# Linear attention in chunks of 64 instead of 128 tokens: scores as four 64x64 array tiles, half the mask, states by one scan

## The chip, the cores and the metric

The kernel runs on one core of a Trainium2 chip, in fp32. The metric is the device time of one execution in microseconds (us). Wherever a ratio is given, it is the mean time of a kernel's fast runs over the mean of the unchanged kernel's fast runs of the same rounds on the same chip, with a 95% interval; it is therefore not quite the ratio of the medians quoted beside it.

## The reference, cut to what matters

```python
# attention: 4 batches, 8 heads, 768 tokens, 48 columns a head
f = 1.0 / (1.0 + np.exp(-f_logit))
for t in range(S):
    state = f[:, :, t, :, None] * state + np.einsum('bhd,bhe->bhde', k[:, :, t], v[:, :, t])
    y[:, :, t] = np.einsum('bhd,bhde->bhe', q[:, :, t], state)
# the heads side by side are x (4, 768, 384); the mixer follows
h = xt @ U @ V                                   # along the tokens, rank 32
u = x + h.transpose(0, 2, 1)
ch = np.maximum(u @ w_ch1, 0.0) @ w_ch2          # 384 -> 1536 -> 384
return u + ch
```

The kernel cuts the tokens into chunks. Inside a chunk the recurrence is a masked product (scores, then inner product); between chunks a 48x48 state is carried on. Gates enter as running products: keys are multiplied by a product X that is scanned backwards over the chunk, queries by its inverse-like Y.

## The kernel before: what the change and the argument touch

Two heads of one batch make a unit; there are 16 units, four to a batch. A unit's work on TensorE comes in pieces, and the pieces of a later batch are dealt out between the mixer's matmuls of the batch before. The kernel is written in one order, and a scheduler fixes at build time in which order the instructions stand on each engine; an engine then takes its list in that order.

```python
C = P                                   # 128 tokens a chunk; NCH = 6 chunks

def scores(g):                          # g = 0, 1: three chunks each
    for c in range(G):
        for par in range(2):            # the two heads
            nc.tensor.matmul(sc[:, par, c * C : (c + 1) * C],
                lhsT=T["k"][rows[par], chunk[g * G + c]], rhs=T["q"][rows[par], chunk[g * G + c]], ...)
    nc.vector.tensor_tensor(T["A"][...], sc[...], causal..., ALU.mult)        # mask

def states():
    ...                                 # 10 products of 128 tokens into ds
    nc.vector.tensor_tensor(st, ds[...], T["whole"]..., ALU.mult)
    for c in range(2, NCH):             # one small update per chunk
        nc.vector.scalar_tensor_tensor(st[:, c - 1, :], st[:, c - 2, :], T["whole"][:, c : c + 1], st[:, c - 1, :], ...)

def read():                             # y = q . state, then y += A . v, both in one piece
    ...

# gates of a later batch: transposed by VectorE, then two sigmoids on ScalarE
turned(fT, r["f"])
nc.scalar.activation(by_chunk[:, :, 1:C], fv[:, :, 1:C], AF.Sigmoid)
nc.scalar.activation(f0, fv[:, :, 0], AF.Sigmoid)

# mixer, first product: relu on ScalarE; pm is one of two PSUM buffers
nc.scalar.activation(z[a, i], pm[:, 0:HALF], AF.Relu)

order = [gates, kept, keep, keys, scores, states, read_back, queries, scores2, read]
```

(Cuts are marked by dots. `kept` transposes the keys, `read_back` scans Y, `keep` scans X.)

## Time and profile before

| what, kernel before | value |
|---|---|
| median of 4 runs | 589.89 us (589.7 to 591.07) |
| profiled run: span, mean granted TensorE clock | 589.1 us, 0.953 |
| first long second-layer piece of the mixer (end of the first stage) | starts at 114.96 us |
| first low-rank piece of the 2nd, 3rd, 4th mixer | 198.01, 336.38, 464.38 us |
| stretches between these marks, and to the end | 83.1, 138.4, 128.0, 124.7 us |
| TensorE's wait for relu, whole run | 16.3 us (12.6 before first-layer, 3.7 before second-layer matmuls) |

The marks cut the run into stretches that can be compared between kernels, since each mark stands for the same work (before the first one, 72 first-layer matmuls of the mixer and units 0 to 3 are done in every kernel; of unit 4 about 0.9 us of pieces, not always the same ones). The second and third stretch hold the same work too, four units and one mixer each, with other preparation on VectorE beside it; yet one is 10 us longer than the other.

### The profile page before, as it was taken

What the parts mean: (1) busy time and instruction counts of PE and PEld (TensorE: products, weight loads), DVE (VectorE), ACT (ScalarE), POOL (GpSimd) and SP (SyncE); (2) the same over time, 40 slices, a digit from 0 to 9 for tenths busy, and PEclk for the clock granted to TensorE, in tenths of its full rate; (3) what the DMA queues carried; (4) which work ended last, traced back from release to release, by engine and by line L of the source; (5) the groups of instructions that cost most, each with busy time, mean ns of one, the idle gap of its engine ahead of it and who ended that gap; (6) DMA issues with size and microseconds to landing.
All of it is one profiled execution on the core that took longest, in us unless ns stands there. A gap on an engine that the chain in (4) does not pass through costs nothing.

```text
span 589.1 us, 8824 instructions
## 1 busy us (share of the span) xinstructions
PE 550.6 (93%) x3737; PEld 344.2 (58%) x3737; DVE 244.8 (42%) x367; ACT 121.8 (21%) x260; POOL 62.4 (11%) x59
## 2 busy tenths in 40 slices
PE   5798897799989999989969999999999999999996
PEld 4687553457656556646645556566566555555553
DVE  5768769826697340638361620254211020000000
ACT  2233346502322103210112102120022003201200
POOL 2111125500022000113020200022000000000000
PEclk9557799999999999989998999999999999999998
DMA  9699827614652135133340310010000000000000
GB/s 167 145 225 177 189 59 208 150 35 104 164 128 54 43 83 132 42 79 94 100 107 0 87 41 13 1 21 14 28 1 1 15 13 14 1 13 27 2 14 31
DMA packets 75295, 41.56 MB, mean 71 GB/s; under 512 B 65774, under 2 KB 68846, under 8 KB 75246
## 3 DMA queue, kind: packets, MB, share of 16 engines
q1 hardware_dynamic: 75246, 40.91, 29.7%
q8 instruction: 31, 0.51, 0.4%
q14 instruction: 18, 0.15, 0.1%
HBM read 36.18 MB, written 4.72 MB: 69 GB/s over the span
## 4 chain that ended last, share of the span: by engine, by line
PE 80%; DVE 11%; DMA 3%; SPq 2%; ACT 1%; issue 1%; POOL 0%; DVEq 0%; ACTq 0%; POOLq 0%
PE po L158 32%; PE pz L149 26%; PE sc L404 5%; PE y L467 4%; PE pu L133 3%; PE pt L326 3%; DVE w_y L62 2%; DMA w_raw<-in_moe_V_dram 2%; PE y L458 2%; PE ds L430 2%; PE put L142 2%; DVE w_y L63 1%; SPq L232 1%; DVE X L358 1%; DVE Y L375 1%
## 5 line engine op out<-in xcount | busy, mean ns | idle before, releaser
L149 PE MATMUL pz<-uT,w 128*128 128x384 f32 x576 | 199.2, 497 | 13.1 <-ACT z L152 12.6
L158 PE MATMUL po<-w,z 128*128 128x384 f32 x576 | 192.2, 492 | 3.7 <-ACT z L152 3.7
L149 PEld LDWEIGHTS pz<-uT,w 128*128 128x128 f32 x576 | 106.3, 191 | 85.7 <-ACT z L152 12.9
L158 PEld LDWEIGHTS po<-w,z 128*128 128x128 f32 x576 | 109.0, 191 | 80.6 <-issue 5.9
L161 DVE TENSOR_TENSOR o<-x,po 128x384 f32<-128x384 f32 x24 | 13.3, 555 | 204.7 <-PE po L158 204.7
L152 ACT ACTIVATE z<-pz 128x384 f32<-128x384 f32 x96 | 46.8, 489 | 167.0 <-PE pz L149 167.0
L410 DVE TENSOR_TENSOR A<-sc,causal 128x768 f32<-128x768 f32 x32 | 30.3, 947 | 63.2 <-PE sc L404 63.2
L358 DVE TENSOR_TENSOR_SCAN X<-fz,ends 128x768 f32<-128x768 f32 x16 | 28.1, 1755 | 33.1 <-ACT fz L347 23.9
L341 POOL TENSOR_TENSOR kT<-kT,X 128x768 f32<-128x768 f32 x8 | 14.6, 1820 | 243.4 <-DVE kT L307 243.4
L404 PE MATMUL sc<-qT,kT 48*128 48x128 f32 x384 | 38.9, 312 | 0.2 <-DVE kT L338 0.2
L404 PEld LDWEIGHTS sc<-qT,kT 48*128 48x128 f32 x384 | 29.6, 204 | 14.2 <-issue 11.2
L467 PE MATMUL y<-v_nat,A 128*64 128x48 f32 x768 | 31.0, 245 | 0.0
L64 POOL TENSOR_TENSOR w<-w_y,w_r 128x384 int32<-128x384 int32 x24 | 23.9, 995 | 65.1 <-DVE w_y L63 65.1
L375 DVE TENSOR_TENSOR_SCAN Y<-fz,starts 128x768 f32<-128x768 f32 x16 | 28.1, 1756 | 5.8 <-POOL qT L341 5.2
L467 PEld LDWEIGHTS y<-v_nat,A 128*64 128x64 f32 x768 | 28.5, 159 | 1.7 <-issue 0.3
L473 ACT COPY x<-y 128x576 f32<-128x576 f32 x16 | 10.2, 636 | 61.2 <-PE y L467 61.2
L458 PE MATMUL y<-st,qT 48*64 48x48 f32 x640 | 18.0, 242 | 5.0 <-DVE st L441 3.6
L144 ACT COPY uT<-put 128x384 f32<-128x384 f32 x24 | 10.7, 480 | 53.7 <-PE put L142 53.7
L458 PEld LDWEIGHTS y<-st,qT 48*64 48x64 f32 x640 | 13.9, 149 | 13.0 <-issue 5.0
L62 DVE TENSOR_SCALAR w_y<-w_y 128x384 uint32<-128x384 uint32 (+1 forms) x27 | 20.3, 752 | 0.7
L133 PE MATMUL pu<-h,V 128*128 128x384 f32 x48 | 19.4, 514 | 0.8 <-DVE x L134 0.8
L341 POOL TENSOR_TENSOR qT<-qT,Y 128x768 f32<-128x768 f32 x8 | 17.2, 2156 | 17.8 <-DVE X L365 11.7
(61 smaller groups left out, 338.0 us busy)
## 6 DMA issues: line engine op xcount, KB each, us to landing
w_raw<-in_moe_w_ch_dram SPq DMA_DIRECT2D x24, 384.0 KB, 3.7
v_nat<-in_v_dram SPq DMA_DIRECT2D x32, 144.0 KB, 2.8
out_dram<-o SPq DMA_DIRECT2D x24, 192.0 KB, 1.9
f_raw<-in_f_logit_dram SPq DMA_DIRECT2D x31, 142.0 KB, 3.1
k_raw<-in_k_dram SPq DMA_DIRECT2D x31, 142.0 KB, 3.4
q_raw<-in_q_dram SPq DMA_DIRECT2D x31, 142.0 KB, 3.3
f_raw<-in_f_logit_dram SPq DMA_DIRECT2D x16, 144.0 KB, 4.9
k_raw<-in_k_dram SPq DMA_DIRECT2D x16, 144.0 KB, 5.0
```

The costliest lines, as they stand in the source:

```text
L62: nc.vector.tensor_scalar(y, y, 3, 0x3FFFFFFF, ALU.logical_shift_left, ALU.bitwise_and)
L133: nc.tensor.matmul(pm[:, 0:DM], lhsT=V[:, t * P : (t + 1) * P], rhs=h[0], start=True, stop=True)
L149: nc.tensor.matmul(pm[:, 0:HALF], lhsT=w1[:, m, i * P : (i + 1) * P], rhs=uT[a][:, m, :], start=(m == 0), stop=(m == NDC - 1))
L152: nc.scalar.activation(z[a, i], pm[:, 0:HALF], AF.Relu)
L158: nc.tensor.matmul(pm[:, 0:DM], lhsT=z[a, i][:, s * P : (s + 1) * P], rhs=w2[:, i, :], start=(i == 0), stop=(i == NFC - 1))
L341: nc.gpsimd.tensor_tensor(t, t, T[of], ALU.mult)
L358: nc.vector.tensor_tensor_scan(backwards(X, S - 1, S), backwards(f, S, S), backwards(ends, S - 1, S), 0.0, ALU.mult, ALU.add,)
L375: nc.vector.tensor_tensor_scan(Y, f[:, 0:S], starts, 0.0, ALU.mult, ALU.add)
L404: nc.tensor.matmul(sc[:, par, c * C : (c + 1) * C], lhsT=T["k"][rows[par], chunk[g * G + c]], rhs=T["q"][rows[par], chunk[g * G + c]], sta ...
L410: nc.vector.tensor_tensor(T["A"][:, :, g * G : (g + 1) * G, :], sc[:, :, 0 : G * C].rearrange("p h (c i) -> p h c i", i=C), causal.unsquee ...
L458: nc.tensor.matmul(o(a, par, c), lhsT=T["q"][rows[par], c * C + a * HC : c * C + (a + 1) * HC], rhs=T["st"][rows[par], c - 1, :], start=(c ...
L467: nc.tensor.matmul(o(a, par, c), lhsT=T["A"][:, par, c, halves[a]], rhs=vt[:, c, par, :], start=False, stop=True, skip_group_check=True,)
```

## The change

The intent: a chunk of 64 tokens halves the masked triangle, so the scores take half the multiplications, and 64x64 tiles of the array work four at a time. More chunks mean more states, so the per-chunk updates are replaced by a single VectorE scan with the chunks innermost. The order in which pieces are handed over changes as well, and the inner product becomes a piece of its own. The product for the chunk states (`ds`) also leaves the two PSUM buffers (the memory that TensorE writes to) that it shared with the mixer.

```diff
-    C = P
+    C = P // 2
...
+            whole = wholes[n % 2]                         # first chunk's factor is 0: the scan restarts there
+            nc.vector.tensor_tensor(whole[:, 1:NCH], T["f0"][:, 1:NCH], X0[:, 1:NCH], ALU.mult)
+            nc.scalar.copy(T["whole"], whole.unsqueeze(1).broadcast_to((P, D, NCH)))
...
+            for c in range(NBL):                          # scores: four tiles
+                for par in range(2):
+                    for s in range(2):
+                        nc.tensor.matmul(sc[part[s], par, c * C : (c + 1) * C],
+                            lhsT=T["k"][rows[par], chunk[2 * c + s]], rhs=T["q"][rows[par], chunk[2 * c + s]], ...)
...
-            ds = ps_mm.tile([P, 512], F32, name="ds", tag="mm")       # one of the mixer's two PSUM buffers
+            ds = ps_big.tile([P, 2, 512], F32, name="ds", tag="big")
...
-            for c in range(2, NCH):
-                nc.vector.scalar_tensor_tensor(st[:, c - 1, :], ...)
+            nc.scalar.copy(d[:, 1:]..., ds[...])          # "added", chunks innermost
+            nc.vector.tensor_tensor_scan(st, d[:, 0 : D * NCH], T["whole"]..., 0.0, ALU.add, ALU.mult)
+            T["st"] = st.rearrange("p (e c) -> p c e", c=NCH)
...
+            seen = two.tile([P, 2], F32, name="seen")     # read, then a small copy that inner waits for
+            nc.scalar.copy(seen, y[:, :, (NBL - 1) * D])
+        def inner():
+            for c in reversed(range(NBL)):
+                for par in range(2):
+                    for s in range(2):                    # two tiles, on the diagonal
+                        nc.tensor.matmul(o(s, par, c), lhsT=T["A"][part[s], par, c, :], rhs=vt[part[s], c, par, :], ...)
...
-                order = [gates, kept, keep, keys, scores, states, read_back, queries, scores2, read]
+                order = [gates, kept, keep, keys, states, scores, read_back, read, queries, inner]
```

(Comments are added here; lines are joined and cut.)

## The prediction

> **What bounds the kernel now.** I read the page's busy shares and slices first, then a table of windows, then the order of TensorE's work, and last the stage before 115 us. Slices of TensorE, VectorE and granted clock:
>
> ```profile
> PE 550.6 (93%) x3737; PEld 344.2 (58%) x3737; DVE 244.8 (42%) x367; ACT 121.8 (21%) x260; POOL 62.4 (11%) x59
> ...
> PE   5798897799989999989969999999999999999996
> ...
> DVE  5768769826697340638361620254211020000000
> ...
> PEclk9557799999999999989998999999999999999998
> ```
>
> From slice 8 on TensorE is full. The windows put numbers to it (window, length, busy time by engine, clock, DMA share, GB/s):
>
> ```profile
> 26.00:52.00 26.00, 23.50 (x298) 19.50 (x300) 19.81 (x39) 8.70 (x19) 3.58 (x4) 0.63 1.11 224
> 52.00:74.00 22.00, 19.81 (x244) 14.69 (x244) 16.90 (x31) 8.32 (x19) 3.40 (x4) 0.74 0.87 166
> ...
> 86.00:113.00 27.00, 20.72 (x62) 10.82 (x60) 26.04 (x43) 17.41 (x38) 13.51 (x14) 1.00 0.74 195
> 113.00:208.00 95.00, 91.61 (x790) 58.02 (x789) 56.59 (x73) 17.59 (x39) 10.92 (x7) 1.00 0.34 82
> 208.00:346.00 138.00, 131.32 (x899) 79.61 (x898) 61.88 (x74) 24.45 (x53) 16.04 (x8) 0.98 0.31 80
> 346.00:474.00 128.00, 128.00 (x900) 78.23 (x898) 31.82 (x52) 19.98 (x40) 7.25 (x4) 1.00 0.04 13
> ```
>
> There are three stages. Up to 74 us the first four units (two heads each) alternate between TensorE at a low clock and VectorE. From 86 to 113 us VectorE converts weights without a pause (26.04 of 27 us). From 113 to 474 us TensorE sets the pace, and units 4 to 15 lie there as small pieces between mixer matmuls; after 474 us there is no attention. So in the long stage only TensorE time counts, and VectorE work removed there is worth nothing by itself. The order of one unit in it, in TensorE's own timeline (start, length, line, output and inputs, tile, count):
>
> ```profile
> 430.39 0.80 PE L458 MATMUL y<-st,qT 48*64 48x48 f32 x40
> 431.12 1.61 PE L467 MATMUL y<-v_nat,A 128*64 128x48 f32 x48
> 432.65 2.20 PE L149 MATMUL pz<-uT,w 128*128 128x384 f32 x6
> 434.79 0.53 PE L422 MATMUL pt<-ident,kT 64*128 64x64 f32 x10
> 435.25 2.20 PE L149 MATMUL pz<-uT,w 128*128 128x384 f32 x6
> 437.38 0.94 PE L404 MATMUL sc<-qT,kT 48*128 48x128 f32 x12
> 438.25 2.20 PE L149 MATMUL pz<-uT,w 128*128 128x384 f32 x6
> 440.38 0.79 PE L430 MATMUL ds<-v_nat,kb 128*64 128x48 f32 x20
> 441.10 0.48 PE L404 MATMUL sc<-qT,kT 48*128 48x128 f32 x2
> 441.51 2.20 PE L149 MATMUL pz<-uT,w 128*128 128x384 f32 x6
> ```
>
> I take a piece's cost from its start to the next start, as ends overlap: read through the state 0.73 us, inner product 1.53, key transposes 0.46, six of twelve score products 0.87 (so 1.74 for all), chunk states 0.72. Together 5.18 us a unit. Every fp32 product is two instructions (384 score instructions are 16 units x 12 products x 2).
>
> **What the skill says.** "TensorEngine Tiling (Array Packing)", Key Properties: different tiles can load weights and multiply in parallel, and a change of tiling mode drains the engine. Both show: six mixer matmuls run in 1.94 us when more of them follow (24 in 7.74), but take 2.13 us (435.25 to 437.38) ahead of a tiled piece, and two score instructions alone cost 0.41 us. "TensorE: Matmul & The Clock Gate", LDWEIGHTS (loading the stationary operand), says that a load's time goes with its columns, at 1.2 columns a ns. The trace agrees with the first, not with the figure: the inner product, two column tiles across all 128 rows, needs 1.53 us for 48, or 26.7 ns each after some 0.25 us of switching, which is 0.42 ns a column of a 64-column load. At half clock the same x48 takes 2.73 and x24 takes 1.45 us: 53 ns each, twice as much. "PSUM — Partial Sum Buffer", PSUM bank collisions raise a hardware error, quotes that different row tiles cannot use one bank at the same time; no row of before tests it. "SBUF — State Buffer", Door 1 (its note on cachelines), says that fp32 reads a line apart (16 bytes) pay a penalty; before reads contiguously, so no run shows it yet.
>
> **A rule for pieces.** A moving column takes 0.84 ns (384 in 322 ns; a 128-column transpose 108 ns). A piece costs about 0.2 us of switching plus, for each instruction, the larger of two: load columns x 0.42 ns over the row halves that load in parallel, and moving columns x 0.84 ns over the tiles in parallel. It returns what is measured: score group 12 x max(27, 54) + 0.2 = 0.85 (0.87); states 20 x 26.7 + 0.2 = 0.73 (0.72); read 40 x max(13.4, 10) + 0.2 = 0.74 (0.73); key transposes 10 x 27 + 0.2 = 0.47 (0.46).
>
> **The change part by part, TensorE, one unit at full clock.**
> Scores: 24 products of 64x64, so 48 instructions on four tiles, 64 moving columns: max(13.4, 13.4) ns. 48 x 13.4 + 0.2 = 0.85 us for 1.74: saves 0.89.
> Inner: still 48 instructions, but 64x64 on the two diagonal tiles: the loads go in two row halves (13.4), the multiplications on two tiles (48 x 0.84 / 2 = 20). 48 x 20 + 0.2 = 1.17 for 1.53: saves 0.36.
> States: twelve chunks instead of five, 48 instructions for 20, on four tiles instead of two: 48 x 13.4 + 0.2 = 0.85 for 0.72: costs 0.13.
> Read: 44 instructions for 40, 0.79 us if nothing else changes. But the state is now read 48 bytes apart; if a moving column takes twice as long it is 44 x 20 + 0.2 = 1.08. I take 0.95, between the two: costs 0.22.
> Key transposes (one instruction each): 12 for 10 at 27 ns: 0.52 for 0.46, costs 0.06.
> Sum 4.34 for 5.18: 0.84 us a unit, and over twelve units in the long stage 10.1 us. The number of separate pieces stays five (read and inner part, the two score groups join), so the drains on the mixer's side stay. The split of the second score group (two ahead of a mixer piece, ten after) occurs some five times in the long stage at about 0.4 us; one score piece may lose it: 1 us as an expectation.
>
> **VectorE, ScalarE.** Removed: one mask of 0.947 us, one product of 0.401 and four updates of 0.266 (2.41 in all); added: one scan of 576, sized from 768 in 1.755 us as about 1.35. VectorE wins 1.06 us a unit. ScalarE gets a broadcast copy of 576 (about 0.63), a copy of 576 out of PSUM (0.65 to 1.2, strided), a token copy (0.2) and a slightly longer key copy: some 1.7 us a unit, 27 us in all, for an engine at 21%.
>
> **Before 115 us.** Here TensorE's clock was 0.50 from 30 to 40 us, and the chain of waits runs through it:
>
> ```profile
> 31.51 1.58 PE sc L404 x12
> 33.09 1.24 PE ds L430 x20
> 34.33 1.47 PE pt L326 x6
> 35.80 1.58 PE sc L404 x12
> ```
>
> Tiled pieces double at that clock, so unit 1 wins about twice the figure above, some 2 us. Unit 0 ends in a wait on a transfer of V (the chain shows 11.3 us of it), so I count nothing there. Units 2 and 3 have VectorE on the chain: 1.06 us less each, but the scan now waits for two copies of ScalarE behind the small products (about 0.5 us), plus a cheaper inner product. About 1.2 each. Sum 4.5 us. The weight conversion from 86 us starts that much earlier, as its transfers wait for VectorE and not the reverse (the queue waited 32.6 us for VectorE's conversion), so the gain carries through.
>
> **What is given back.** Before, the chunk updates ran beside other TensorE work. Now states, copy, scan (0.7 + 1.35 + 0.15 us) must end before the read, with one score piece (0.85) as sure cover: 1.4 us of wait where no mixer piece falls between. That is only while the long 24-matmul pieces are handed out, when several calls pass without any: I expect two such units, 2.8 us, and some three short waits of 0.4 us for the token copy and the mask ahead of inner. Before lost about 0.5 us in two units likewise (read 1.19 instead of 0.73). Net 3.2 us.
>
> **Sum.** 589.8 - 10.1 - 1 - 4.5 + 3.2 = 577.4; I say 577.5 us.
>
> **Rivals.** First: the diagonal tiles of inner write one bank from two row halves. If the hardware serialises them, each instruction takes 40 ns: 2.1 us instead of 1.17, 0.95 us a unit more, about 13 us over the kernel: 590, no change. The outputs are on different partitions, which speaks against it. Second: small pieces are bound by issue, not by the array. 48 score and 48 state instructions at 18 ns instead of 13.4 cost 0.45 us a unit, 6 us in all: 583. The read of before, 40 instructions in 0.73 us, speaks against it. Third: ScalarE, being in order, holds the mixer's relu behind copies that wait for VectorE. Its present copy of the scan's result already waits 32.5 us in total without much harm (TensorE waited 12.6 us for relu, with two PSUM buffers); the new one waits about 0.4 us longer. I give it 3 us: 580. Fourth, the other way: the strided read is free and no read stalls: 571.
>
> **Range and chances.** The known terms give 577; the rivals reach from 571 to 590 and mostly lie above. The 8-in-10 range is 569 to 587. The 2% mark is 578, close to the estimate: faster 0.52, within 2% 0.42, slower 0.06, the last needing serialised tiles and more waits together.
>
> **What will show it.** In the timeline after: the score piece x48 near 0.85 us (over 1.1 and the issue rival holds), inner x48 near 1.17 (over 1.5 and the bank rival holds), read x44 between 0.8 and 1.1 with the stride, states x48 near 0.85. In the waits: read behind the scan, a few us in total; the relu wait near 13 us. VectorE's busy time should fall by 17 us to about 228, ScalarE's rise to about 149. The first long mixer piece, now at 114.96 us, should start near 110.5. I am wrong if the pieces shrink as computed and the end does not follow, or if the start of that piece does not move.

## The result, and the profile after

The changed kernel takes 571.74 us (median of 4 runs, 570.41 to 572.7) for 589.89 us: ratio 0.9687, 95% interval 0.9662 to 0.9711. It is faster by 3.1%. The range of the prediction holds it; its centre, 577.5, is 5.8 us too high. Measured by profiled spans, 589.1 became 571.0: 18.1 us less.

The busy totals of the changed kernel's page:

```profile
PE 532.8 (93%) x4665; PEld 332.4 (58%) x4665; DVE 231.5 (41%) x287; ACT 145.7 (26%) x308; POOL 61.8 (11%) x64
```

TensorE has 17.8 us less to do, VectorE 13.3 us less, and ScalarE 23.9 us more (forecast: 17 less and 27 more for the last two). The windows of the changed kernel, to be laid beside those of the kernel before:

```profile
113.00:208.00 95.00, 94.95 (x1005) 59.69 (x1004) 57.02 (x64) 23.90 (x53) 11.30 (x8) 1.00 0.39 96
208.00:346.00 138.00, 137.39 (x1201) 83.11 (x1199) 59.16 (x55) 33.31 (x71) 16.08 (x8) 1.00 0.29 77
346.00:474.00 128.00, 126.67 (x1106) 75.94 (x1105) 28.27 (x32) 24.78 (x51) 7.26 (x4) 1.00 0.04 13
```

TensorE is now busy for 94.95 of 95 us and 137.39 of 138, where it had 91.61 and 131.32, and its clock is 1.00 where it was 0.98. So some 9.4 us of idle time went from these two windows (1.75 us of it is the wait that ends at the first mark, 114.96 us). That is a second source of gain beside the smaller pieces, and the prediction has no term for it. (Of the 1.33 us that are missing in the last window, 1.2 are four waits of the last mixer's preparation at 468 to 472 us; in the kernel before they come at 487 to 490 us, behind the window.)

Next, one unit in TensorE's timeline (start, length, line, operation, output and inputs, tile, shape, count):

```profile
413.50 1.60 PE L493 MATMUL y<-v_nat,A 64*64 64x48 f32 x48
415.04 2.20 PE L149 MATMUL pz<-uT,w 128*128 128x384 f32 x6
...
419.82 0.92 PE L447 MATMUL ds<-v_nat,kb 64*64 64x48 f32 x48
420.67 2.20 PE L149 MATMUL pz<-uT,w 128*128 128x384 f32 x6
422.80 0.93 PE L417 MATMUL sc<-qT,kT 48*64 48x64 f32 x48
423.66 2.20 PE L149 MATMUL pz<-uT,w 128*128 128x384 f32 x6
425.79 1.23 PE L475 MATMUL y<-st,qT 48*64 48x48 f32 x44
426.95 0.91 PE L149 MATMUL pz<-uT,w 128*128 128x384 f32 x2
```

From start to next start, states take 0.85 us and scores 0.86, both as forecast (0.85). The read takes 1.16 instead of 0.95, and the inner product 1.54 instead of 1.17: its old length (1.53).

Then the idle time. On the page, the group of the mixer's first-layer matmuls ends with the idle time ahead of it and what ended most of that. Kernel before:

```profile
L149 PE MATMUL pz<-uT,w 128*128 128x384 f32 x576 | 199.2, 497 | 13.1 <-ACT z L152 12.6
```

Changed kernel:

```profile
L149 PE MATMUL pz<-uT,w 128*128 128x384 f32 x576 | 199.7, 497 | 6.2 <-ACT z L152 5.3
```

The prediction expected this wait to stay near 13 us or to grow by 3. It fell to 5.3, and no wait for relu is left after 113 us (the 3.7 us ahead of the second-layer matmuls are gone too). The largest of those that went lies in the kernel before at 309 us; here its timeline across engines:

```profile
306.09 2.06 DVE L307 STREAM_TRANSPOSE fT<-f_raw 128x768 f32<-128x768 f32 x1
308.19 0.84 ACT L353 ACTIVATE fz<-fT 128x762 f32<-128x762 f32 x1 [6.56 <-DVE fT L307]
308.93 0.47 ACT L152 ACTIVATE z<-pz 128x384 f32<-128x384 f32 x1
309.46 3.66 PE L149 MATMUL pz<-uT,w 128*128 128x384 f32 x6 [4.71 <-ACT z L152]
```

Read it from below. TensorE stood still for 4.71 us because both PSUM buffers of the mixer were full and relu had not emptied one. Relu had its input, but ScalarE's list had the sigmoid of the next unit's gates in front of it, and ScalarE had been idle for 6.56 us waiting for that sigmoid's input, a transposition that VectorE reached late. And the pause cost more than itself: the six matmuls after it took 3.66 us, at a granted clock of 0.58, where six ahead of a tiled piece otherwise take 2.20. The kernel before has two more such waits behind its first stage, of 1.64 us (at 176 us) and 1.96 us (at 257 us). After the second of these, 24 second-layer matmuls took 9.70 us instead of 8.01, at a clock of 0.82. That is 8.3 us of waiting and 3.2 us of slow work behind it, 11.5 us in all. (At 176 us it was not a sigmoid that stood in front of the relu but `least`, a small copy of the scan X that waited for the scan.) The changed kernel at the same place, on ScalarE:

```profile
308.03 0.48 ACT L152 ACTIVATE z<-pz 128x384 f32<-128x384 f32 x1
...
309.94 0.83 ACT L362 ACTIVATE fz<-fT 128x756 f32<-128x756 f32 x1 [1.43 <-DVE whole L377]
```

Here relu stands ahead of the sigmoid. Nothing in the diff asks for that. It was the first thing to test.

### The profile page after: what moved, and what is told of

Its sections match the earlier page's. It is cut to its first block, busy times and chain, and to the rows that moved or that the text cites. A ratio compares the mean times of both kernels' runs of the same rounds, so it can differ in the third digit from the quotient of the medians.

```text
span 571.0 us, 10691 instructions
## 1 busy us (share of the span) xinstructions
PE 532.8 (93%) x4665; PEld 332.4 (58%) x4665; DVE 231.5 (41%) x287; ACT 145.7 (26%) x308; POOL 61.8 (11%) x64
## 4 chain that ended last, share of the span: by engine, by line
PE 79%; DVE 10%; DMA 2%; SPq 2%; ACT 2%; issue 2%; POOL 1%; POOLq 0%; DVEq 0%; ACTq 0%
PE po L158 33%; PE pz L149 27%; PE y L493 4%; PE pu L133 3%; PE y L475 3%; PE pt L335 2%; PE ds L447 2%; DMA f_raw<-in_f_logit_dram 2%; DVE X L367 2%; PE sc L417 2%; DVE Y L386 2%; PE put L142 1%; DVE w_y L62 1%; SPq L233 1%; DVE kT L316 1%
## 5 line engine op out<-in xcount | busy, mean ns | idle before, releaser
L161 DVE TENSOR_TENSOR o<-x,po 128x384 f32<-128x384 f32 x24 | 13.3, 554 | 206.9 <-PE po L158 206.9
L152 ACT ACTIVATE z<-pz 128x384 f32<-128x384 f32 x96 | 46.4, 489 | 125.7 <-PE pz L149 125.7
L460 DVE TENSOR_TENSOR_SCAN st<-added,whole 128x576 f32<-128x576 f32 x16 | 21.6, 1351 | 58.8 <-ACT added L454 58.8
L475 PE MATMUL y<-st,qT 48*64 48x48 f32 x704 | 21.0, 272 | 14.4 <-DVE st L460 10.9
L493 PEld LDWEIGHTS y<-v_nat,A 64*64 64x64 f32 x768 | 28.3, 156 | 7.8 <-issue 3.2
L493 PE MATMUL y<-v_nat,A 64*64 64x48 f32 x768 | 30.4, 241 | 0.2
L475 PEld LDWEIGHTS y<-st,qT 48*64 48x64 f32 x704 | 18.2, 165 | 19.7 <-issue 19.7
L144 ACT COPY uT<-put 128x384 f32<-128x384 f32 x24 | 10.9, 483 | 49.7 <-PE put L142 49.7
L447 PEld LDWEIGHTS ds<-v_nat,kb 64*64 64x64 f32 x768 | 14.1, 135 | 10.4 <-issue 7.3
L59 ACT ACTIVATE w_y<-w_raw 128x384 f32<-128x384 f32 (+1 forms) x27 | 14.8, 549 | 16.6 <-POOL w L64 9.3
```

The source lines that it names most:

```text
L447: nc.tensor.matmul(ds[par * PAD : (par + 1) * PAD, s, c * D : (c + 1) * D], lhsT=T["kb"][part[s], par, c, :], rhs=vt[part[s], c, par, :], ...
L475: nc.tensor.matmul(o(c % 2, par, c // 2), lhsT=T["q"][rows[par], chunk[c]], rhs=T["st"][rows[par], c, :], start=(c <= 2), stop=False, skip ...
L493: nc.tensor.matmul(o(s, par, c), lhsT=T["A"][part[s], par, c, :], rhs=vt[part[s], c, par, :], start=False, stop=True, skip_group_check=True,)
```

## The experiments

Theories for the 18.1 us. **Tiles**: the smaller pieces won it, as the prediction computes, and something else closed the gap. **Schedule**: the change moved the scheduler's order, which took the relu waits away, and the tile arithmetic won less than forecast. Then smaller questions: why the read and the inner product are too long, and why the first stage won so little (113.73 for 114.96 us; the forecast was 110.5).

| run | what it is | median us | ratio (95%) |
|---|---|---|---|
| x1 | before, with the changed order of pieces | 584.22 | 0.987 (0.984 to 0.990) |
| x2 | before, sigmoid of the gates held back | 577.83 | 0.976 (0.973 to 0.979) |
| x3 | changed, state read contiguously (wrong result) | 570.19 | 0.964 (0.961 to 0.967) |
| x4 | changed, state scan ahead of the Y scan | 573.72 | 0.970 (0.967 to 0.973) |
| x5 | changed, half the moving columns in inner (wrong) | one look | |
| x6 | changed, inner's outputs in two banks (wrong) | one look | |
| x7 | changed, sigmoid held back | 571.56 | 0.966 (0.962 to 0.969) |
| x8 | x7, state first in early units, state copied | 569.03 | 0.961 (0.957 to 0.964) |
| x9 | changed, 48 stationary columns in inner (wrong) | one look | |
| x10 | changed, once more | 573.72 | 0.971 (0.968 to 0.974) |
| x11 | x7 with the state copied only | 570.9 | 0.964 (0.961 to 0.968) |
| x12 | x11, state first in all units | 575.5 | 0.973 (0.970 to 0.976) |

The kernel before had medians of 591.69 (x1 to x4), 591.65 (x5 to x8) and 590.84 us (x9 to x12) beside them. The kernels marked wrong give a wrong result, because only the length of one piece was wanted of them.

### x1: the order of the pieces alone

The kernel before keeps its chunks of 128, but hands its pieces over in the changed order.

```diff
-                order = [gates, kept, keep, keys, scores, states, read_back, queries, scores2, read]
+                order = [gates, kept, keep, keys, states, scores, read_back, read, queries, inner]
```

(`scores` does both groups here, and `read` is split into read and inner.)

> The kernel before with its chunks of 128, where only the order of one unit's pieces is that of the changed kernel: states, both score groups, backward scan, read through the state, queries, inner products. Piece theory (the 18 us come from smaller TensorE pieces): 589 to 591 us, nothing gained. Schedule theory (they come mostly from waits of the mixer's matmuls for their relu, 8.3 us idle in three places plus about 3.5 us of lowered clock after two of them, which vanished because ScalarE's and VectorE's instructions came out in another order): 577 to 582 us, and the TensorE idle ahead of the mixer's matmuls after 113 us under 2 us.

Measured: 584.22 us, ratio 0.987, so some 7.5 us less, a miss of what was expected by 2 us. The waits for relu behind the first mark (114.23 us) fell from 8.3 to 3.6 us, not under 2; none is longer than 1.85. From the first mark to the end the run is 6.3 us shorter. No tile was changed, but the score groups are joined here too: in the second stretch the tiled pieces take 0.8 us less. So order alone brings about half of what the relu waits cost (12.2 us by x2), not all of it.

### x2: the gates' sigmoid held where it was written

The kernel before, with one thing changed: the two sigmoids of later batches are held to their place in program order, so that the scheduler can't move them ahead of relus written earlier.

```diff
-            nc.scalar.activation(by_chunk[:, :, 1:C], fv[:, :, 1:C], AF.Sigmoid)
-            nc.scalar.activation(f0, fv[:, :, 0], AF.Sigmoid)
+            tc.keep_in_program_order(nc.scalar.activation(by_chunk[:, :, 1:C], fv[:, :, 1:C], AF.Sigmoid))
+            tc.keep_in_program_order(nc.scalar.activation(f0, fv[:, :, 0], AF.Sigmoid))
```

> The kernel before with one thing changed: from the third batch on the sigmoid of the gates stays in program order on ScalarE, so it cannot stand ahead of a relu that TensorE waits for. Schedule theory: the two long waits (4.7 and 2.0 us) and the lowered clock after each are gone, 578 to 581 us. Piece theory: 589 to 591 us. If holding the sigmoid delays the forward scan, a wait of TensorE for it shows up instead, and the time stays.

Measured: 577.83 us, ratio 0.976. The window of the stretch that had 6.7 us of idle TensorE:

```profile
208.00:346.00 138.00, 138.00 (x931) 83.77 (x930) 60.08 (x75) 24.01 (x51) 14.55 (x8) 1.00 0.30 79
```

TensorE is busy for all 138 us. No matmul waits for relu after the start of the first long piece. Its marks are 114.49, 195.63, 323.83, 451.84 and 576.4 us, so the stretches are 81.1, 128.2, 128.0 and 124.6: the second has lost its 10 us and is now as long as the third. From the first long piece to the end, 474.1 us became 461.9: 12.2 us, against the 11.5 us counted above from waits and slow clock. The schedule theory holds, and it is the larger part: two calls on two instructions of the old kernel bring two thirds of what the whole change brought (by the ratios, 2.4 of 3.1%).

### x7: the same hold in the changed kernel

The same two lines in the changed kernel.

> The changed kernel with the gates' sigmoid held in program order on ScalarE from the third batch on, as in the run that held them in the kernel before (ratio 0.976 there). Schedule theory: in the changed kernel the waits for a relu are already small (about 1.5 us after 113 us), so at most 2 us are won: ratio 0.965 to 0.970. The ratio of this run to that one is then the worth of the tile part alone: 0.990 to 0.994 (3.5 to 6 us).

Measured: 571.56 us, 0.966, with its interval over that of the changed kernel (0.9687). The hold wins nothing that is clear of noise, because the changed kernel's own order had already put relu first. (The trace shows about 1 us: the second stretch takes 125.7 instead of 126.7 us. In the changed kernel the token copy `seen` stands behind the sigmoid twice, and TensorE's loads for the inner product wait 0.73 us for it, at 241.03 and 310.88 us; with the hold it runs at once.) Beside x2 it also measures what the change brings when the gates are held in both kernels: 0.9656 over 0.9758 is 0.9895, so about 1.05%, or 6 us. Each ratio is known to about 0.3%, so this is 6 us give or take 2; from the first mark to the end the traces show 5.9.

### x3: does the strided read of the state cost?

The changed kernel, with the state read as if its 48 columns lay side by side, instead of 48 bytes apart.

```diff
-            T["st"] = st.rearrange("p (e c) -> p c e", c=NCH)
+            T["st"] = st.rearrange("p (c e) -> p c e", c=NCH)
```

> The changed kernel with the read through the state taking 48 neighbouring values instead of values 48 bytes apart (a wrong result on purpose; the same instructions, tiles and waits). If the stride makes the read's moving operand slow: read of 44 from 1.17 to 0.79 us at full clock, 12 units x 0.38 = 4.6 us in the long stage and perhaps 1 us before it, 566 to 568 us. If the read is bound by something else (issue, bank sharing): read stays at 1.17 and the time at 571 to 572 us.

The result is wrong (relative error 0.40). TensorE's timeline:

```profile
161.06 0.90 PE L475 MATMUL y<-st,qT 48*64 48x48 f32 x44
161.90 0.88 PE L335 MATMUL pt<-ident,q_raw 128*128 128x128 f32 x6
```

The piece takes 0.84 us instead of 1.17. With 0.25 us for the change of mode, an instruction has 21 ns with the stride and 13.4 without, so the stride, and nothing else, makes the read long. At half clock (0.50 granted, in the first stage) the piece takes 1.45 us to the next start with and without the stride: there it costs nothing. In total 570.19 us, 0.964. The changed kernel did not run in these rounds, so the total is not compared; by the marks (112.82, 191.41, 317.67, 442.59 us) the three stretches with units are 2.8 us shorter than the changed kernel's, where 0.33 us in twelve units would be 4.0. That was less than expected of it, and the total of 566 to 568 us was missed.

### x5, x6, x9: why the inner product did not get shorter

Three theories for 1.53 instead of 1.17 us. The multiplications could set it (then half the moving columns shorten it), the common PSUM bank of the two diagonal tiles could (then two banks shorten it), or the loading of the stationary columns.

x5 moves 24 columns instead of 48:

```diff
-                            o(s, par, c), lhsT=T["A"][part[s], par, c, :], rhs=vt[part[s], c, par, :],
+                            y[part[s], par, c * D : c * D + (D // 2 if c else D)], lhsT=T["A"][part[s], par, c, :],
+                            rhs=vt[part[s], c, par, 0 : (D // 2 if c else D)],
```

> The changed kernel with the inner products of chunks 2 to 11 of a head taking 24 moving columns instead of 48 (a wrong result on purpose; the first two chunks keep 48 so that the whole output is written). The inner piece of 48 instructions measured 1.53 us where the forecast was 1.17. If weight loads of the two diagonal tiles go one after the other (64 columns x 0.42 ns = 26.7 ns each): it stays at 1.5 us. If the multiplications or writes into one shared bank set it: 0.25 + 8 x 26.7 + 40 x 13.4 ns = 1.0 us.

Its timeline:

```profile
168.63 1.60 PE L493 MATMUL y<-v_nat,A 64*64 64x24 f32 x48
```

The next piece starts at 170.16 us, so this one still takes 1.53 us. The multiplications do not set it. (The granted clock is 1.00 here in all three looks, so the pieces can be compared although the state of these runs is unknown.)

x6 puts the outputs of the second 64 tokens into the other bank:

```diff
-                return y[part[s], par, c * D : (c + 1) * D]
+                return y[part[s], (par + s) % 2, c * D : (c + 1) * D]
```

> The changed kernel with the outputs of the second 64 tokens of each pair put into the other bank (the heads of those tokens are exchanged, a wrong result on purpose), so that the two diagonal tiles of the inner products never write one bank at once. Bank theory: inner piece from 1.53 to about 1.17 us at full clock. Load theory: it stays at 1.5 us. The read through the state then has its row tiles in shared banks: if sharing costs, it rises above 1.17 us.

Its timeline:

```profile
168.48 1.60 PE L493 MATMUL y<-v_nat,A 64*64 64x48 f32 x48
170.01 2.20 PE L149 MATMUL pz<-uT,w 128*128 128x384 f32 x6
```

Again 1.53 us. The bank is not the cause, although the prediction had said that a piece over 1.5 us would mean just that. The second test of this run agrees: the read, whose row tiles now share banks, still takes 1.17 us (164.57 to 165.74).

x9 takes 48 instead of 64 stationary columns, and keeps the 24 moving ones:

```diff
-                            o(s, par, c), lhsT=T["A"][part[s], par, c, :], rhs=vt[part[s], c, par, :],
+                            y[s * C : s * C + (48 if c else C), par, c * D : c * D + (D // 2 if c else D)],
+                            lhsT=T["A"][part[s], par, c, 0 : (48 if c else C)],
+                            rhs=vt[part[s], c, par, 0 : (D // 2 if c else D)],
```

> As the run with half the moving columns, where the inner piece stayed at 1.53 us, so neither multiplications nor banks set it; now those products also load 48 stationary columns instead of 64 (40 of the 48 instructions; wrong result on purpose). If the loads of the two diagonal tiles go one after the other at 0.42 ns a column: 0.25 + 8 x 26.7 + 40 x 20 ns = 1.26 us. If each instruction holds its tile for a fixed 53 ns whatever its columns (two tiles in turn: 26.7): it stays at 1.53 us.

Its timeline:

```profile
168.34 1.33 PE L493 MATMUL y<-v_nat,A 64*48 64x24 f32 x48
169.61 2.20 PE L149 MATMUL pz<-uT,w 128*128 128x384 f32 x6
```

1.27 us, where 1.26 was expected. Forty of the 48 instructions have 16 columns fewer, and 0.26 us over 640 columns is 0.41 ns for each. So the load of stationary columns sets this piece, at 26.7 ns for each load of 64 columns, and not a fixed time per instruction, and the move from two tiles of 128 rows to two of 64 rows left that as it was.

What that means for the rule is argued, not shown. The runs fit two readings: either the loads of the two diagonal tiles go one after the other at 0.42 ns a column, or each tile takes 0.84 ns a column and the tiles in use work side by side. The second needs no exception for the other products: with two tiles in use a load of 64 columns comes every 26.7 ns (inner, in both kernels; states before), with four every 13.4 ns (scores and states after; the read when contiguous), and both are 53.4 ns a tile. It doesn't fit the key transposes, which load 128 columns into each of two tiles every 27 ns. The run that would separate the two, an inner product spread over all four tiles, was not made.

### x4: the first stage

The read waits for the state's scan. This is the first stage of the changed kernel, VectorE and TensorE in one timeline:

```profile
45.17 1.76 DVE L386 TENSOR_TENSOR_SCAN Y<-fz,starts 128x768 f32<-128x768 f32 x1
46.85 1.33 DVE L460 TENSOR_TENSOR_SCAN st<-added,whole 128x576 f32<-128x576 f32 x1
48.33 1.52 PE L475 MATMUL y<-st,qT 48*64 48x48 f32 x44 [3.84 <-DVE st L460]
```

The next unit's scan of Y stands ahead of the state's scan, so TensorE waits 3.84 us. Over the run these waits are 10.9 us, in three places, all before 115 us (in the kernel before, the read waits 3.2 us for the state in the same three units). x4 puts the Y scan behind the state's scan of the unit before by a dependency:

```diff
+            if n - 1 in scanned:
+                behind(ins, scanned[n - 1])
...
+            scanned[n] = nc.vector.tensor_tensor_scan(
```

> The changed kernel with VectorE's state scan held ahead of the next unit's backward scan. In the changed kernel TensorE waits 3.2 to 3.8 us for the state scan in each of units 1 to 3, and its clock falls to half for what follows. If that order is what ate the gain forecast for the stage before 115 us: these waits fall by about 1.7 us each, the first long mixer piece starts some 4 to 5 us earlier than at 113.73, total 566 to 568 us. If that stage is bound by the loop of all engines together, or by the weight conversion after it: start within 1.5 us of 113.73, total 570 to 572 us.

Measured: 573.72 us, 0.970: the same as the changed kernel, and not the 566 to 568 us expected. The three waits fell from 10.9 to 6.1 us, and the first stage's attention ended 3.7 us earlier (first low-rank piece at 64.83 instead of 68.53 us). The first mark moved from 113.73 to 106.66 us, although the last two of those matmuls then waited until 114.88 for a weight; the second mark moved by 3.7 us, from 193.67 to 189.99. But the stretch after that mark took 129.2 instead of 126.7 us, with three waits for relu of some 0.9 us again, and at the end next to nothing of the gain was left. So the order of the two scans is shown to be the cause of the first stage's small gain, and the cure moved the order elsewhere.

### x8, x11, x12: a version that beats both

x8 joins what had worked: the held sigmoids, the state first only in the units of the first stage, and from the fifth unit on a copy on GpSimd that lays the state out contiguously, for the read. Its result is correct.

```diff
+            if n - 1 in scanned and n < HP:
+                behind(ins, scanned[n - 1])
...
+            if n >= HP:
+                flat = d[:, 1:].rearrange("p (c e) -> p c e", c=NCH)
+                nc.gpsimd.tensor_copy(flat, T["st"])
+                T["st"] = flat
```

> A correct kernel meant to beat both: the changed kernel with the gates held, the state scan ahead of the backward scan in the first units only, and from unit 4 on the state copied by GpSimd into neighbouring values, so that the read runs at the contiguous 0.84 us. Expected: 4 us from the read, 3.5 us from the first stage (which the run with the state scan first everywhere won there and lost again to later waits), 0 to 1 from the held gates: ratio 0.954 to 0.959, 563 to 566 us. If GpSimd's copy comes too late the read waits for it, and most of the 4 us go.

Measured: 569.03 us, 0.961 (0.957 to 0.964). It misses what was expected of it, and it is the lowest correct time; its interval overlaps that of x11, and that of x7 at its edge. TensorE waited 1.8 us for the new copy, in three places. The first stage brought only 1.7 us at the first mark, where 3.5 were expected, and the edit says why: `n < HP` leaves out unit 4, whose Y scan (57.87 us) still stands ahead of the state's scan of unit 3 (59.54 us), so one of the three waits stays at 3.84 us.

x11 is x8 without any change of VectorE's order:

> The changed kernel with the gates held and the state copied by GpSimd into neighbouring values from unit 4 on, without any change to VectorE's order. The read at 0.84 instead of 1.17 us gives 12 x 0.33 = 4 us, less about 0.6 us where the copy is waited for (three times in the combined run): 3 us under the changed kernel of this job, ratio 0.961 to 0.964.

Measured: 570.9 us, 0.964, beside 573.72 us for the changed kernel in the same rounds. So the hold and the contiguous read together bring about 3 us, about as expected. By the marks of x7 and x11 the hold has a good part of it: the three stretches with units take 331.2 us in x7 and 330.4 in x11, so there the contiguous read wins 0.8 us net of the waits for the copy (1.9 us).

x12 has the state first in every unit, not only in the early ones:

> As the run before it, and the state scan held ahead of the backward scan in every unit (the gates are held too, so the late waits that ate this gain in the earlier run should not come back). Expected 2 to 4 us under the run before it: ratio 0.955 to 0.960. If the first stage gives nothing by this: the same time as the run before it.

Measured: 575.5 us, 0.973, a clear miss. TensorE waits 7.6 us for the copy on GpSimd, up to 3.2 us at once. The copy itself got slower. In x11, and then in x12:

```profile
280.77 1.20 POOL L466 COPY added<-st 128x576 f32<-128x576 f32 x1 [9.36 <-DVE st L460]
281.29 2.57 POOL L476 COPY added<-st 128x576 f32<-128x576 f32 x1 [13.46 <-DVE st L470]
```

In x12 VectorE's next instruction is the Y scan, and the copy runs beside it: eleven of the twelve copies take about 2.6 us there. The one without a Y scan beside it takes 1.21, and in x8 and x11, where none has one beside it, all twelve take about 1.2. What the two engines share was not tested.

### x10: the changed kernel again

> The changed kernel itself, as the reference of this job: ratio 0.966 to 0.971 to the kernel before, as on record.

Measured: 573.72 us, 0.971 (0.968 to 0.974), on another chip than x1 to x8. It agrees with the first comparison (0.9687), and the two intervals overlap. Differences of 0.3% between batches of runs are therefore not read here.

## Why the prediction was right or wrong

Direction and range were right. But two errors stood against each other, and the sum of 18.1 us has another make-up than the forecast of 12.4. That the centre is off by no more than 5.8 us is luck: the terms it did forecast brought about 5.8 us (-4.6 and -1.2 in the table), which alone would have given some 584 us, not 577.5 and not faster by 2%.

| part | forecast us | measured us, from the marks |
|---|---|---|
| smaller pieces in the long stage | -10.1 and -1 | -4.6 (changed against x2) |
| first stage | -4.5 | -1.2 |
| given back by new waits, long stage | +3.2 | about 1 for `seen`, inside the -4.6; none for the scan |
| relu waits and the slow clock behind them | not in the sum | -12.2 (x2 against before) |
| sum | -12.4 | -18.0 |

**Steps that held.** Scores (0.86 for 0.85 us), states (0.85), key transposes (0.51 for 0.52), the size of the scan (1.351 for 1.35 us) and the added ScalarE work (23.9 for 27 us). The issue rival falls with the scores and states.

**The term that was missing.** "Its present copy of the scan's result already waits 32.5 us in total without much harm (TensorE waited 12.6 us for relu, with two PSUM buffers)" is where the prediction had the answer before it and passed on. It took the relu wait for a constant of the kernel, to which the change could only add ("I give it 3 us"). The runs show that most of it in the long stage was an accident of order, worth 12.2 us with the slow clock behind it: x2 removes it on the old kernel by holding two instructions, x1 removes about half of it by the order of pieces, and the changed kernel has none left behind its first stage, with the hold or without it. The window in the prediction's own fence, 131.32 us of work in 138, was the trace of it, and so were digits in its row of slices: "From slice 8 on TensorE is full" passes over an 8, an 8 and a 6 in slices 11, 17 and 20 (counted from 0), and these are the three waits. Which part of the change, beyond the order of pieces, moved the remaining waits was not isolated. One candidate was not tested: `ds` left the mixer's two PSUM buffers. In x1, where it still uses them, `ds` itself waits 0.4 us for a relu.

**The inner product, 1.17 forecast, 1.53 measured.** The failed step is "the loads go in two row halves (13.4)". They came every 26.7 ns, as before (x5 and x9). Its halving over the row halves rested on the read (four tiles) and the key transposes (two row halves of 128 columns), and no piece of the kernel before had two tiles on the diagonal to test it. The bank rival's sign, over 1.5 us, came true by a hair, but its own figure was 2.1 us and its cause is not the cause (x6).

**The read, 0.95 forecast, 1.17 measured.** The prediction had put the full stride at 1.08 and taken the middle to "free". The stride costs its full price at full clock (x3), and slightly more than reckoned.

**The saving per unit.** Forecast 0.84 us. Measured over the second stretch, x2 against x7: all tiled pieces of four units take 23.51 us before and 20.57 after, so 5.87 and 5.14 a unit: 0.73. The base was also too low. 5.18 us had come from one cleanly cut unit, but before, the two score groups were cut into 14 pieces in four units, at 8.95 us; after, they are 4 pieces, at 3.30. So the joining of pieces won more than the 1 us that it was given, and that hid most of the loss at the inner product and the read. Twelve units at 0.73 would be 8.8 us; from the first mark on the traces show 4.6 (5.9 with x7). The stretches say where the rest is. Units 8 to 15 do win 2.9 us for each four. Units 4 to 7 win only 1.4 us together, since there the kernel before cuts its scores less (8 pieces, 1.85 us a unit) and reads in 0.73 us throughout. The mixer's own pieces take 1.2 us more over the three stretches, and `seen` costs the changed kernel another 1 us against x7.

**The first stage, 4.5 forecast, 1.2 measured.** The terms for units 2 and 3 reckoned 0.5 us for the wait of the scan on ScalarE's copies. What came was 10.9 us of waiting of the read for the scan, because the Y scan stood ahead of it (x4 shows that cause; before, the read waited 3.2 us in these units).

**What is given back.** The 2.8 us for reads that stall in the long stage did not appear there: all such waits lie in the first stage. The token copy `seen` held inner at 241.03 and 310.88 us for 0.7 us each.

## What to carry to other kernels

Before crediting a change with the arithmetic of its pieces, list every wait on the engine that sets the pace, and ask of each whether it comes from the data or from the place of an instruction in another engine's list; the second kind can vanish or appear with any edit. To tell them apart, hold one instruction in place on the old kernel and measure: here that explained two thirds of the gain, and a cure that was right locally (x4, x12) lost its gain to something that it set off elsewhere. And a pace fitted to tiles in one arrangement is not known for another until that arrangement has been run.

## What the Trainium skill lacked or had wrong

- "TensorEngine Tiling (Array Packing)", Key Properties, says that different tiles can load weights and multiply in parallel, but gives no rate at which loads follow each other by arrangement. The runs show 13.4 ns a load of 64 columns with four tiles in turn and 26.7 ns with two, on the diagonal (1.53 us for 48, unchanged with half the moving columns, 1.27 with 48 stationary columns) as well as in two column halves.
- "TensorE: Matmul & The Clock Gate", LDWEIGHTS (loading the stationary operand), gives 1.2 columns a ns and doesn't say how it adds up over tiles. The prediction called this wrong, at 0.42 ns a column. If each tile loads by itself, 64 columns in 53.4 ns are the page's figure; no run here tells this reading from loads that follow each other twice as fast. At half clock the loads take twice as long (53 for 26.7 ns, inner product before).
- "SBUF — State Buffer", Door 1, says that reads that go to a new line each time pay a penalty, without a figure for TensorE. Here a moving operand 48 bytes apart made a piece 1.17 instead of 0.84 us at full clock, and 1.45 us with and without it at half clock.
- "PSUM — Partial Sum Buffer", PSUM bank collisions raise a hardware error, quotes for two TensorE writes that row tiles must not share a bank, and then measures the collision only where they share the bank and the 32 partitions too. The changed kernel's inner product writes one bank from two row halves to different partitions: the results are correct, and two banks make it no faster (1.53 us both). Whether two such writes ever fall at the same moment isn't shown.
- No page that bears on this tells how much the order of instructions on ScalarE and VectorE, fixed at build time, can cost TensorE: 12.2 us of 589 here, in waits of 1.6 to 4.7 us, two of them followed by 1.5 and 1.7 us lost to slow matmuls.
